# An attention and mixer kernel: pair tiles of the Strassen tail become single PSUM banks, its row additions come in halves, and the order is planned anew

## The chip, the cores and the metric

One core of a Trainium2 chip runs the whole program. The metric is the device time of one execution in microseconds (us). TensorE (PE) multiplies matrices, VectorE (DVE), ScalarE (ACT) and GpSimd (POOL) work element by element, and SyncE (SP) issues all DMA transfers from one queue.

## The reference

Attention with a decay over 64 heads (8 batches of 8 heads, 576 positions, 64 columns), then a mixer over tokens and one over channels:

```python
scores = q @ k.T / sqrt(64) + (cum[i] - cum[j])      # cum: running sum of log(clip(f)); causal
x = softmax(scores) @ v                              # heads side by side: 8 x 576 x 512
u = x + (relu(x.T @ w_tok1) @ w_tok2).T              # 576 -> 256 -> 576
out = u + relu(u @ w_ch1) @ w_ch2                    # 512 -> 1536 -> 512
```

All of it is in 32-bit floats. The kernel splits each operand into a high and a low part of a shorter format (fp32r) and sums three products (high by high, low by high, high by low), so every product of the reference is three matmuls.

## The kernel before, in words

The program has three stages. In **attention** (up to about 560 us) each head's scores are multiplied, reduced, exponentiated, normalised, transposed and multiplied with v, with the token mixer and a first part of the channel mixer woven in. The **conventional part** (to about 693 us) does the channel mixer for 1,024 of the 4,608 tokens. The **tail** does the other 3,584 tokens in four steps of 896 (the function `big`, step s = 0 to 3): each step uses a form of Strassen's scheme in which seven products take the place of eight, once for the way up (512 to 1,536 columns, less the 256 that attention has done) and once for the way down. A product up (the loop over `UP`, L1522 to L1524) has five groups (`pr`) of six matmuls of 448 columns into one PSUM bank each; ACT copies the sum out (L1533), or DVE adds it to a row (L1539). A product down (the function `product`, L1584 to L1586) has five groups of six matmuls: three go to the first half m = 0 of its result and three to the second half m = 1, and the two halves lie in two banks. DVE adds the result to a row of the output in SBUF (L1608, 896 columns; L1604 for the two halves of the very last product). The products of a chain (`CHAIN`) add up in the same banks.

PSUM has eight banks, called b0 to b7 here. b0 and b1 make the tile `pair0`, b2 and b3 `pair1`; attention uses them for scores, results of v and sums. b4 to b7 are the single tiles `bank4` to `bank7` of attention. When attention's single tiles are done, `swapp` lays `pair2` and `pair3` over them. In the tail a sum of the way up is one half of a pair tile (kind `x1`), and a result of the way down is a whole pair tile (kind `x2`). A semaphore wait is placed for a tile, as the framework sees it: a write to a pair tile follows the reads of that pair tile.

The order of the work is not written by hand. A planner (`Plan.run`) simulates the engines with a cost for each operation, and at each moment takes the ready operation of lowest priority number; the numbers stand in the tables `PR`, `OFF`, `STEP` and the like. Its choices fix the order on every engine and which bank each result gets. `dma` gives a transfer a cost on SP's queue (`dur`) and a rate (bytes per ns). Where the plan leaves PE idle, the last loop of the kernel adds small idle matmuls (L783, 16 columns, the operand is the constant `lower`); 120 of them stand at the start:

```python
for _ in range(PRM["FILL"] if at_ == 0 else int((gap - GAP[0]) / GAP[1]) if gap > GAP[2] else 0):
    E["idle"](at_ == 0)
```

At the start SP loads the first heads' q and k (`xt<-in_qk`, L962, for the first four heads, which lie in a tile named xt, and `raw<-in_qk`, L925, for later ones), the decay input (`xt<-in_f`, L751) and the token mixer's weights (`dd<-in_w_tok`, L798). The decay passes DVE and ACT (L752 to L757), and its rows go by DMA beside q and k (`xt<-cc`, L947); the scores (L985) read both.

Of the kernel before, what the change touches and what calls it, by code (L numbers as in the profile page):

```python
# [13 lines left out]
ALU = mybir.AluOpType  # L14
# [9 lines left out]
    k0=(2,),  # L24
    k1=(3,),
# [6 lines left out]
    k8=(1,),  # L32
    k9=(3,),
    k10=(4, 5, 6, 7, 8, 9,),
    k11=(6, 2, 4, 7, 8, 14, 16, 18, 22, 28, 32, 40, 41, 42, 43, 46, 62, 59, 53, 57, 63, 78, 77, 79, 80, 95, 112, 110, 111, 109, 126, 469, 470, 472, 471, 473, 481, 480, 478, 477, 479, 487, 486, 485, 484, 488, 493, 495, 494, 496, 498, 502, 499, 501, 500, 503, 506, 505, 507, 510, 512, 517, 515, 516, 518, 520,),
    k12=(2, 3, 6, 8, 11, 15, 20, 27, 33, 36, 46, 50, 56, 78, 101, 106, 161, 910, 912, 929, 930, 940, 941, 949, 950, 958, 960, 964, 969, 972, 982, 987, 991, 994, 998,),
    k13=(4, 5, 8, 11, 18, 20, 30, 32, 41, 46, 56, 70, 68, 93, 137, 115, 194, 983, 986, 1001, 1003, 1013, 1015, 1024, 1025, 1034, 1038, 1044, 1052, 1055, 1061, 1064, 1069, 1073, 1078,),
    k14=(6, 7, 9, 14, 19, 21, 39, 38, 45, 48, 58, 74, 72, 98, 171, 138, 200, 985, 988, 1004, 1005, 1014, 1017, 1032, 1030, 1036, 1040, 1045, 1054, 1059, 1063, 1065, 1070, 1074, 1079,),
    k16=(4, 5, 9, 13, 18, 19, 35, 34, 39, 40, 53, 66, 65, 98, 156, 906, 905, 915, 918, 935, 936, 947, 946, 959, 956, 961, 963, 967, 977, 984, 988, 989, 992, 996, 1001,),
    k17=(10, 11, 12, 13, 14, 19, 27, 26, 28, 30, 35, 51, 48, 61, 97, 981, 979, 999, 998, 1011, 1012, 1021, 1019, 1035, 1031, 1041, 1046, 1048, 1058, 1062, 1066, 1067, 1071, 1076, 1081,),  # L40
    k18=(12, 19, 48, 61, 72, 74, 89, 106, 120, 136, 154, 169, 181, 192, 206, 222, 240, 249, 266, 283, 295, 309, 315, 336, 347, 362, 384, 388, 399, 420, 433, 444,),
    k19=(10, 11, 20, 15, 21, 23, 34, 36,),
    k20=(0, 5, 27, 33,),
    k21=(0, 2, 1, 5, 4, 3, 11, 13, 9, 22, 18, 23, 30, 29, 25, 38, 36, 35, 49, 50, 53, 59, 60, 57, 75, 80, 77, 89, 93, 90, 103, 104, 106, 114, 116, 115, 135, 137, 134, 144, 151, 146, 170, 168, 167, 184, 181, 187, 198, 200, 201, 217, 214, 216, 227, 229, 228, 240, 242, 241, 260, 264, 262, 277, 276, 275, 293, 295, 292, 305, 315, 312, 324, 330, 327, 342, 343, 345, 359, 362, 361, 371, 380, 373, 389, 392, 394, 406, 408, 403, 421, 420, 425, 437, 440, 438, 453, 454, 456, 469, 466, 470, 487, 489, 485, 498, 500, 499, 522, 517, 519, 538, 533, 537, 553, 555, 551, 565, 569, 568, 579, 585, 600, 605, 607, 606, 618, 623, 621, 632, 644, 637, 653, 668, 658, 675, 673, 670, 700, 697, 702, 705, 709, 704, 723, 720, 722, 739, 742, 735, 760, 763, 762, 766, 764, 772, 799, 797, 800, 807, 813, 805, 817, 820, 831, 833, 837, 828, 847, 861, 860, 863, 862, 875, 880, 892, 889, 901, 896, 902, 915, 918, 922, 929, 925, 931, 949, 948, 951, 961, 964, 952,),
# [413 lines left out]
    ),  # L458
)
F1 = PRM["F1"]  # L460

QUADS = ("11", "12", "21", "22")
HW = 256
GAP = (300, 85, 700)
HT = 448
CONV = 2


def dd_units(a, n):
    return tuple(("dd", i) for i in range(a, a + n))  # L470
# [207 lines left out]
def build(nc, env, dims):  # L678
# [32 lines left out]
    def at(b):  # L711
        return env[b.kind][b.slot]
# [1352 lines left out]
```

## Time and profile before

| what | before |
|---|---|
| median of 3 runs | 1051.08 us (1050.98 to 1052.93) |
| profiled execution, its time | 1053.12 us |
| profiled execution, its span (first to last instruction) | 1050.0 us |
| PE busy in the span | 1030.5 us (98%) |
| DVE, ACT, POOL busy | 77%, 66%, 40% |
| granted TensorE clock, mean | 0.996 |

The span is what the instructions cover; 3.1 us lie around it in the profiled execution. A matmul's record begins when it starts and ends with a modelled end, and neighbours overlap, so the start of the next one tells how fast PE goes. The granted clock is a share of 2.4 GHz: 1.00 is that level, 0.50 is 1.2 GHz.

### The profile page before, as it was taken

To read this page: it belongs to the slowest core of one execution; us is meant where nothing else is said; L and a number is where in the kernel's file an instruction comes from. 1 tells how busy PE (TensorE), PEld (TensorE's weight loads), DVE (VectorE), ACT (ScalarE), POOL (GpSimd) and SP (SyncE) were. 2 spreads that over 40 slices of the span, in tenths; PEclk is the share of its full clock that TensorE was granted. 3 is DMA by queue.
4 is the path that set the end of the run, shared out by engine and by line. 5 is a ranking of instruction groups with operands and counts; after the bars stand their busy time and mean duration, and the time that the engine had idled before them with its cause. 6 is when DMAs were issued, how large, how long until landed. Compare 5 with 4: busy or idle time off the path is not lost.

```text
span 1050.0 us, 19792 instructions
## 1 busy us (share of the span) xinstructions
PE 1030.5 (98%) x6481; PEld 928.9 (88%) x6481; DVE 807.1 (77%) x1943; ACT 689.3 (66%) x1719; POOL 419.2 (40%) x528
## 2 busy tenths in 40 slices
PE   8999999999999999999999999999999999999998
PEld 6678999999999999999999888889898888989897
DVE  5788888888888777888899995456966875786594
ACT  5788888788788878888997542235446544643552
POOL 5478868778788585987942000000000000000000
PEclk9999999999999999999999999999999999999999
DMA  7766657465655545555548845052683284277044
GB/s 216 223 232 212 227 184 235 176 210 187 204 196 196 203 175 173 199 190 200 214 149 274 291 158 184 10 179 82 201 267 114 89 253 150 93 243 226 1 162 158
DMA packets 101605, 192.59 MB, mean 183 GB/s; under 512 B 14032, under 2 KB 45520, under 8 KB 100480
## 3 DMA queue, kind: packets, MB, share of 16 engines
q1 hardware_dynamic: 101504, 191.34, 54.6%
q8 instruction: 51, 0.84, 0.3%
q14 instruction: 50, 0.41, 0.1%
HBM read 100.16 MB, written 37.49 MB: 131 GB/s over the span
## 4 chain that ended last, share of the span: by engine, by line
PE 88%; ACT 4%; DVE 4%; issue 1%; DMA 1%; POOL 1%; SPq 0%; DVEq 0%; ACTq 0%; POOLq 0%
PE bank L1041 10%; PE bank L985 6%; PE pair L1584 5%; PE pair L1585 5%; PE pair L1586 5%; PE pair L1522 5%; PE pair L1524 5%; PE pair L1523 5%; PE pair L985 3%; PE pair L1123 3%; PE pair L1125 3%; PE bank L1256 2%; PE pair L1277 2%; PE bank L1258 2%; PE bank L1257 2%; PE pair L1279 2%
## 5 line engine op out<-in xcount | busy, mean ns | idle before, releaser
L1027 POOL TENSOR_SCALAR pr<-pr,rec 128x448 f32<-128x448 f32 (+4 forms) x320 | 165.2, 532 | 69.8 <-DVE rec L1020 35.4
L719 ACT ACTIVATE p<-bank 128x384 fp32r<-128x384 f32 (+3 forms) x300 | 129.9, 473 | 23.4 <-PE bank L1041 20.8
L1041 PE MATMUL bank<-ident,pr 128*128 128x128 f32 (+1 forms) x960 | 141.4, 276 | 0.8 <-DVE ring L731 0.4
L999 ACT ACTIVATE pr<-bank,nmin 64x64 f32<-64x64 f32 (+3 forms) x256 | 118.3, 468 | 24.7 <-DVE nmin L992 21.7
L1041 PEld LDWEIGHTS bank<-ident,pr 128*128 128x128 f32 (+1 forms) x960 | 107.2, 131 | 21.1 <-issue 3.8
L728 DVE TENSOR_TENSOR p<-bank,p 128x384 fp32r<-128x384 f32 (+1 forms) x180 | 106.0, 591 | 18.1 <-ACT p L719 16.7
L992 DVE CUSTOM_DVE_ANT_0 bank<-bank,mask 64x64 f32<-64x64 f32 (+3 forms) x256 | 107.0, 430 | 12.7 <-PE bank L985 8.5
L1584 PE MATMUL pair<-ring,w2r 128*128 128x448 f32 x230 | 84.6, 368 | 2.3 <-ACT ring L719 0.8
L985 PE MATMUL bank<-k 128*128 128x320 f32 (+1 forms) x480 | 84.8, 304 | 0.8 <-DVE low L728 0.4
L1585 PE MATMUL pair<-ring,w2r 128*128 128x448 f32 x230 | 84.2, 366 | 0.0
L1586 PE MATMUL pair<-ring,w2r 128*128 128x448 f32 x210 | 76.9, 366 | 0.0
L1125 PE MATMUL pair<-p,vv 128*128 128x512 f32 x240 | 76.6, 321 | 0.0
L719 ACT ACTIVATE ring<-xt 128x448 fp32r<-128x448 f32 (+2 forms) x100 | 60.1, 612 | 21.4 <-DVE xt L1734 5.1
L911 POOL TENSOR_TENSOR hl<-raw,hl 128x1152 fp32r<-128x1152 f32 x27 | 72.1, 2669 | 1.6
L1123 PE MATMUL pair<-p,vv 128*64 128x512 f32 x240 | 70.0, 332 | 0.0
L985 PEld LDWEIGHTS bank<-k 128*128 128x128 f32 (+1 forms) x480 | 62.1, 176 | 5.1 <-DVE low L728 0.8
L728 DVE TENSOR_TENSOR low<-bank,p 64x512 fp32r<-64x512 f32 (+1 forms) x120 | 52.4, 443 | 14.1 <-ACT p L719 12.5
L999 ACT ACTIVATE pr<-pair,nmin 128x576 f32<-128x576 f32 x64 | 47.2, 738 | 13.3 <-DVE nmin L992 10.7
L725 POOL TENSOR_TENSOR ring<-xt,ring 128x576 fp32r<-128x576 f32 x32 | 46.3, 1456 | 19.5 <-ACT ring L719 19.3
L722 POOL TENSOR_SCALAR p<-low 64x576 fp32r<-64x576 f32 x60 | 40.1, 668 | 31.6 <-DVE low L728 25.6
L992 DVE CUSTOM_DVE_ANT_0 pair<-pair,mask 128x576 f32<-128x576 f32 x64 | 48.9, 764 | 4.3 <-PE pair L985 4.2
L719 ACT ACTIVATE ring<-bank 128x512 fp32r<-128x512 f32 (+2 forms) x96 | 46.9, 497 | 7.2 <-PE bank L1767 3.7
(202 smaller groups left out, 3156.9 us busy)
## 6 DMA issues: line engine op xcount, KB each, us to landing
k<-hl SPq DMA_DIRECT2D x180, 288.0 KB
w2r<-sd SPq DMA_DIRECT2D x80, 256.0 KB
raw<-in_qk SPq DMA_DIRECT2D x60, 288.0 KB
w2r<-qd SPq DMA_DIRECT2D x60, 256.0 KB
vr<-in_v SPq DMA_DIRECT2D x32, 320.0 KB
ud<-xt SPq DMA_DIRECT2D x8, 1152.0 KB
pd<-part SPq DMA_DIRECT2D x32, 288.0 KB
dd<-in_w_ch SPq DMA_DIRECT2D x12, 512.0 KB
```

The source lines that it names most:

```text
L719: nc.scalar.activation(out, in_, func, scale=scale)
L728: nc.vector.tensor_tensor(out, in_, asf(hi), op=ALU.subtract)
L985: nc.tensor.matmul(ps[:m, of : of + w], k[:, 0, i0 : i0 + m], k[:, 1, j0 : j0 + w], start=(x == 0), stop=(fq or x == 1))
L992: nc.vector.tensor_tensor_reduce(x, x, E["mask"][:m, a : a + w], -1.0 / D**0.5, 3e38, op0=ALU.add, op1=ALU.min, accum_out=E["nmin"][sm][:m ...
L999: nc.scalar.activation(at(pr)[:m, poff[t] : poff[t] + w], at(buf)[:m, of : of + w], AF.Exp, bias=E["nmin"][sm][:m, t : t + 1], scale=-1.0, ...
L1027: nc.gpsimd.tensor_scalar(x, x, r, 0.0, op0=ALU.mult, op1=ALU.add)
L1041: nc.tensor.transpose(out, at(pr)[:, poff[i] + start[j] : poff[i] + end[j]], E["ident"])
L1123: nc.tensor.matmul(x[:D], at(vv)[:, v0 + j, :D], at(pb)[:, 1, c0 : c0 + w], start=False, stop=last)
L1125: nc.tensor.matmul(x, at(vv)[:, v0 + j, :], at(pb)[:, 0, c0 : c0 + w], start=False, stop=last)
L1584: nc.tensor.matmul(o_, wh[:, ms], h_, start=first and pr == 0, stop=False, skip_group_check=not first)
L1585: nc.tensor.matmul(o_, wl[:, ms], h_, start=False, stop=False, skip_group_check=not first)
L1586: nc.tensor.matmul(o_, wh[:, ms], l_, start=False, stop=pr == PH - 1, skip_group_check=not first)
```

## The change

PSUM: b4 to b7 stay single tiles for the whole program, and the pair tiles of b0 to b3 are given up after attention's and the conventional part's last use, for four single tiles (`swapp`). All sums of the tail, up and down, now take single banks: a result of the way down has two of them, any two. The first product up of the first step may take b4 to b7 before that exchange (kind `y1`). The DVE addition of a result is two instructions of 448 columns, one for each bank, in place of one of 896. The store to the output stays one transfer, but for the last product.

Planning: the model's transfers begin no earlier than 2,450 ns; a load of later heads' q and k costs 600 ns of SP's queue (before: 400) and moves at 260 bytes per ns (300), and a gather of a head's operand (`k<-hl`, L958) at 330 (300). Idle matmuls planned before 50,000 ns go by their own thresholds (`EARLY`). The priority tables are replaced as a whole, so the order differs everywhere. Cut to its core:

```diff
-GAP = (300, 85, 700)
+GAP, EARLY = (300, 85, 700), (200, 65, 500)
...
-        tail = dma_at = port_at = 0.0
+        tail = port_at = 0.0
+        dma_at = 2450.0
...
-                    n + o["load"], lambda raw=raw, n=n, x=x: nc.sync.dma_start(at(raw)[x::2], E["qk"][n // 2][x * D : x * D + D]), 294912, dur=400, wr=[(raw, x)], bufs=[raw]
+                    n + o["load"], lambda raw=raw, n=n, x=x: nc.sync.dma_start(at(raw)[x::2], E["qk"][n // 2][x * D : x * D + D]), 294912, dur=600, rate=260, wr=[(raw, x)], bufs=[raw]
...
-            dma(n + o["kh"], lambda k1=k1, f=gather: f(at(k1)[0::2], 0, 2), 294912, dur=660, rd=[(hl, 0)], wr=[(k1, 0)], bufs=[k1, hl])
+            dma(n + o["kh"], lambda k1=k1, f=gather: f(at(k1)[0::2], 0, 2), 294912, dur=660, rate=330, rd=[(hl, 0)], wr=[(k1, 0)], bufs=[k1, hl])
...
-                ps = Buf("x1") if first else held_[ch, pr]
+                ps = Buf("y1" if s == 0 and k == 1 and pr < 4 else "x1") if first else held_[ch, pr]
...
-            ps = Buf("x2") if first else held_[ch]
+            ps = [Buf("x1") for _ in (0, 1)] if first else held_[ch]
...
-                        o_ = res(m)
+                        o_ = at(ps[m])[:, :HT]
...
-                        p.op("PE", [mm_(HT)] * 3, pp if m == 0 else pp + L, lambda f=mm, m=m: f((m,)), rd=b + ([ps] if m else []), wr=[(ps, m)] + ([] if m else [ps]), bufs=[ps, *b])
+                        p.op("PE", [mm_(HT)] * 3, pp if m == 0 else pp + L, lambda f=mm, m=m: f((m,)), rd=b, wr=[ps[m]], bufs=[ps[m], *b])
...
-            p.op("DVE", d_dve(T), tk, lambda: nc.vector.tensor_tensor(Rq(to), res(), Rq(to), op=ALU.add), rd=[ps], wr=[R[to]], bufs=[ps, R[to]])
+            for c in (0, 1):
+                p.op(
+                    "DVE", d_dve(HT), tk, lambda c=c: nc.vector.tensor_tensor(Rq(to)[:, c], at(ps[c])[:, :HT], Rq(to)[:, c], op=ALU.add),
+                    rd=[ps[c], R[to]], wr=[(R[to], "o", c)], bufs=[ps[c], R[to]],
+                )
...
-        if any(z.kind == "one" for z in q.bufs):
+        if any(z.kind in ("sc", "av", "acc") for z in q.bufs):
...
 def swapp():
-        ones.__exit__(None, None, None)
-        pairs.extend(pp.tile([P, 1024], F32, name=f"pair{i}") for i in (2, 3))
+        pairp.__exit__(None, None, None)
+        E["x1"] = {**banks, **{(f"b{i}",): pp.tile([P, 512], F32, name=f"bank{i}") for i in range(4)}}
...
+                g0, g1, g2 = GAP if o.start > 50000 else EARLY
+                for _ in range(PRM["FILL"] if at_ == 0 else int((gap - g0) / g1) if gap > g2 else 0):
```

Three places show what the new plan does. The first is SP's queue at the start of the program, before and then after (`xt_135` holds the decay input f, `xt_136` the first heads' q and k, `raw` later heads' q and k, `dd` weights to be decoded):

```order
L962 DMA xt_136<-in_qk 64x1152
L925 DMA raw_157<-in_qk 64x1152
L798 DMA dd<-in_w_tok 64x512
L751 DMA xt_135<-in_f 64x576
L798 DMA dd<-in_w_tok 128x512
L962 DMA xt_136<-in_qk 64x1152
```

```order
L925 DMA raw_157<-in_qk 64x1152
L751 DMA xt_135<-in_f 64x576
L798 DMA dd<-in_w_tok 64x512
L798 DMA dd<-in_w_tok 128x512
L962 DMA xt_136<-in_qk 64x1152
L798 DMA dd<-in_w_tok 64x512
```

The decay input moves from the fourth place to the second, and the first head's q and k from the first to the fifth.

The second place is PE's start: the idle matmuls (L783), then the scores of the first head (one result in a pair tile, two in bank tiles), idle matmuls, the scores of the second head, before and then after:

```order
L783 MATMUL pair_64<-lower 16x128 x87
L985 MATMUL pair_63<-xt_136 128x288 x2
L985 MATMUL bank_68<-xt_136 128x320
L985 MATMUL bank_68<-xt_136 128x192
L985 MATMUL bank_69<-xt_136 64x64
L985 MATMUL bank_69<-xt_136 128x448
L783 MATMUL pair_64<-lower 16x128 x33
L985 MATMUL bank_68<-xt_136 128x320
L985 MATMUL bank_68<-xt_136 128x192
```

```order
L783 MATMUL pair_71<-lower 16x128 x87
L985 MATMUL pair_70<-xt_136 128x288 x2
L985 MATMUL bank_63<-xt_136 128x320
L985 MATMUL bank_63<-xt_136 128x192
L985 MATMUL bank_64<-xt_136 64x64
L985 MATMUL bank_64<-xt_136 128x448
L783 MATMUL pair_71<-lower 16x128 x18
L985 MATMUL bank_65<-xt_136 128x320
L985 MATMUL bank_65<-xt_136 128x192
```

The second head now gets banks of its own, where before it took the first head's again, and 18 idle matmuls stand ahead of it in place of 33; another 23 follow behind it.

The third place is PE's last product, whose two halves m = 0 and m = 1 are added and stored one by one: before, where the first half ends and the second begins, and after, the last three groups of the program:

```order
L1584 MATMUL pair0_63<-ring8_145,w2r3_7248 128x448
L1585 MATMUL pair0_63<-ring8_145,w2r3_7248 128x448
L1586 MATMUL pair0_63<-w2r5_7252,w2r3_7248 128x448
L1584 MATMUL pair0_63<-ring0_137,w2r4_7250 128x448
L1585 MATMUL pair0_63<-ring0_137,w2r4_7250 128x448
L1586 MATMUL pair0_63<-ring10_147,w2r4_7250 128x448
```

```order
L1584 MATMUL bank5_64<-ring1_138,w2r1_6963 128x448
L1585 MATMUL bank5_64<-ring1_138,w2r1_6963 128x448
L1586 MATMUL bank5_64<-w2r7_7267,w2r1_6963 128x448
L1584 MATMUL bank0_8387<-ring3_140,w2r0_6961 128x448
L1585 MATMUL bank0_8387<-ring3_140,w2r0_6961 128x448
L1586 MATMUL bank0_8387<-ring4_141,w2r0_6961 128x448
L1584 MATMUL bank0_8387<-ring1_138,w2r1_6963 128x448
L1585 MATMUL bank0_8387<-ring1_138,w2r1_6963 128x448
L1586 MATMUL bank0_8387<-w2r7_7267,w2r1_6963 128x448
```

Both halves had the tile `pair0`, in two blocks of 15 matmuls; now each half has its own tile, the halves' groups alternate up to there, and the first half ends six matmuls before the program's last.

## Rows read from the trace of the kernel before

**Rows 1.** The page, part 1: busy time (share) and instructions of each engine.

```profile
PE 1030.5 (98%) x6481; PEld 928.9 (88%) x6481; DVE 807.1 (77%) x1943; ACT 689.3 (66%) x1719; POOL 419.2 (40%) x528
```

**Rows 2.** Stretches: length; PE, PEld, DVE, ACT, POOL busy; granted clock; DMA share, GB/s.

```profile
0.00:12.64 12.64, 11.51 (x126) 9.81 (x126) 4.52 (x17) 4.96 (x8) 8.07 (x18) 1.00 0.73 190
...
21.93:28.76 6.83, 6.83 (x20) 4.75 (x20) 4.22 (x16) 3.60 (x12) 2.79 (x6) 0.50 0.98 277
28.76:62.00 33.24, 33.24 (x170) 19.60 (x168) 25.49 (x84) 27.72 (x82) 19.83 (x34) 1.00 0.68 218
62.00:100.00 38.00, 35.02 (x257) 30.20 (x257) 33.12 (x100) 32.27 (x92) 30.63 (x37) 1.00 0.60 211
100.00:560.00 460.00, 458.85 (x3525) 433.44 (x3524) 383.42 (x1116) 384.23 (x1061) 346.94 (x426) 1.00 0.57 198
...
693.17:1046.40 353.23, 346.30 (x1681) 314.04 (x1679) 250.07 (x394) 174.45 (x332) 0.00 (x0) 1.00 0.51 163
```

**Rows 3.** Timeline of the tail near 813: start, length, what [idle before <-releaser].

```profile
811.91 0.62 DVE L1539 TENSOR_TENSOR dd<-pair,dd 128x448 f32<-128x448 f32 x1 [1.23 <-PE pair L1524]
...
812.52 0.36 PE L1523 MATMUL pair<-ring,held 128*128 128x448 f32 x1
...
812.73 0.36 PE L1524 MATMUL pair<-ring,held 128*128 128x448 f32 x1
...
813.52 0.53 ACT L1533 ACTIVATE dd<-pair 128x448 f32<-128x448 f32 x1
...
814.10 0.47 PE L1522 MATMUL pair<-w2r,held 128*128 128x448 f32 x1 [1.01 <-ACT dd L1533]
```

**Rows 4.** Timeline of the tail near 820.

```profile
819.80 0.62 DVE L1539 TENSOR_TENSOR dd<-pair,dd 128x448 f32<-128x448 f32 x1
...
820.87 0.62 DVE L1539 TENSOR_TENSOR dd<-pair,dd 128x448 f32<-128x448 f32 x1
...
821.54 0.47 PE L1522 MATMUL pair<-w2r,held 128*128 128x448 f32 x1 [0.99 <-DVE dd L1539]
```

**Rows 5.** Timeline of the tail near 891.

```profile
890.74 0.55 ACT L1533 ACTIVATE dd<-pair 128x448 f32<-128x448 f32 x1 [1.45 <-PE pair L1524]
...
892.12 0.53 ACT L1533 ACTIVATE dd<-pair 128x448 f32<-128x448 f32 x1
...
892.70 0.47 PE L1522 MATMUL pair<-ring,held 128*128 128x448 f32 x1 [0.78 <-ACT dd L1533]
```

**Rows 6.** Timeline of the tail near 853.

```profile
852.80 1.08 DVE L1608 TENSOR_TENSOR r<-pair,r 128x896 f32<-128x896 f32 x1
...
853.99 0.44 PE L1584 MATMUL pair<-ring,w2r 128*128 128x448 f32 x1 [0.57 <-DVE r L1608]
```

**Rows 7.** Timeline of the last product.

```profile
1043.03 0.62 DVE L1604 TENSOR_TENSOR r<-pair,r 128x448 f32<-128x448 f32 x1 [1.39 <-PE pair L1586]
...
1043.71 0.47 PE L1584 MATMUL pair<-ring,w2r 128*128 128x448 f32 x1 [0.71 <-DVE r L1604]
```

**Rows 8.** Groups of one line, DVE, tail: count, busy, mean ns, idle before.

```profile
L1608 DVE TENSOR_TENSOR part<-pair,part 128x896 f32<-128x896 f32 x16 | 17.4, 1088 | 5.4 <-PE pair L1586 5.4
```

**Rows 9.** Waits of PE in the tail: us in total, times, longest.

```profile
PE pair L1522 <- ACT mask L1533: 0.6, 1, 0.6
...
PE pair L1584 <- DVE h L1539: 0.2, 1, 0.2
```

**Rows 10.** Timeline of the start: SP's issues (SPq) and PE.

```profile
1.37 0.57 SPq L925 DMA_DIRECT2D raw<-in_qk  x1
...
2.62 0.60 SPq L751 DMA_DIRECT2D xt<-in_f  x1
...
6.97 5.67 PE L783 MATMUL pair<-lower 128*16 128x128 f32 x87
...
13.33 1.21 PE L985 MATMUL pair<-xt 66*128 66x288 f32 x4 [0.69 <-DMA xt<-cc]
...
20.45 3.01 PE L985 MATMUL bank<-xt 66*128 66x320 f32 x8 [1.91 <-ACT held L719]
```

More of the change, by code (lines that the diff above doesn't have):

```diff
@@ L23 @@
 PR = dict(
-    k0=(2,),
-    k1=(3,),
+    k0=(1,),
+    k1=(1,),
     k2=(0,),
@@ L1526, in big @@
                 p.op(
-                    "PE", [mm_(HT)] * 6, pp, mm, rd=[*th, *tl, *toks_of(1, pr, blk)] + ([("turn", s)] if k == 1 else []) + ["gatep"] * (first and s == 0),
+                    "PE", [mm_(HT)] * 6, pp, mm, rd=[*th, *tl, *toks_of(1, pr, blk)] + ([("turn", s)] if k == 1 else []) + ["gatep"] * (first and ps.kind == "x1" and s == 0),
                     wr=[ps], bufs=[ps, *th, *tl],
@@ L1600, in product @@
             tk = t2 + L * (n + 1)
             to = {1: "11", 2: "11", 6: "12", 5: "22", 7: "22", 3: "12", 4: "21"}[k]
-            if ends:
-                for c in (0, 1):
-                    p.op("DVE", d_dve(HT), tk, lambda c=c: nc.vector.tensor_tensor(Rq("21")[:, c], res(c), Rq("21")[:, c], op=ALU.add), rd=[(ps, c), R["21"]], wr=[(R["21"], "o", c)], bufs=[ps, R["21"]])
-                    dst = E["outT"][(2 + c) * P : (3 + c) * P, t0 : t0 + HT]
-                    dma(tk, lambda c=c, dst=dst: nc.sync.dma_start(dst, Rq("21")[:, c]), P * HT * 4, rd=[(R["21"], "o", c)], bufs=[R["21"]])
-                return
@@ L1879, in attn_mixer_kernel @@
     const = ctx.enter_context(tc.tile_pool(name="const", bufs=1))
-    pairs = [psum.tile([P, 1024], F32, name=f"pair{i}") for i in range(2)]
-    ones = tc.tile_pool(name="ones", bufs=1, space=bass.MemoryType.PSUM)
-    op_ = ones.__enter__()
+    banks = {(f"b{i}",): psum.tile([P, 512], F32, name=f"bank{i}") for i in range(4, 8)}
+    E["one"] = E["y1"] = banks
+    pairp = tc.tile_pool(name="pairs", bufs=1, space=bass.MemoryType.PSUM)
+    pp = pairp.__enter__()
+    pairs = [pp.tile([P, 1024], F32, name=f"pair{i}") for i in range(2)]
     E["sc"] = {("b0", "b1"): pairs[0]}
@@ L1886, in attn_mixer_kernel @@
     E["acc"] = {(f"b{i}",): pairs[i // 2][:, (i % 2) * 512 : (i % 2) * 512 + 512] for i in range(4)}
-    E["one"] = {(f"b{i}",): op_.tile([P, 512], F32, name=f"bank{i}") for i in range(4, 8)}
     def swapp():
-        ones.__exit__(None, None, None)
-        pp = ctx.enter_context(tc.tile_pool(name="pairs", bufs=1, space=bass.MemoryType.PSUM, reuse_waits="tile"))
-        pairs.extend(pp.tile([P, 1024], F32, name=f"pair{i}") for i in (2, 3))
-        E["x1"] = {(f"b{i}",): pairs[i // 2][:, (i % 2) * 512 : (i % 2) * 512 + 512] for i in range(8)}
-        E["x2"] = {(f"b{2 * i}", f"b{2 * i + 1}"): x for i, x in enumerate(pairs)}
+        pairp.__exit__(None, None, None)
+        pp = ctx.enter_context(tc.tile_pool(name="lasts", bufs=1, space=bass.MemoryType.PSUM, reuse_waits="tile"))
+        E["x1"] = {**banks, **{(f"b{i}",): pp.tile([P, 512], F32, name=f"bank{i}") for i in range(4)}}
     E["swapp"] = swapp
@@ L2023, in attn_mixer_kernel @@
         for o in order:
-            heads = heads and not any(x.kind in ("acc", "dA", "dB", "x1", "x2") for x in o.bufs)
+            heads = heads and not any(x.kind in ("acc", "x1", "y1") for x in o.bufs)
             if o.eng == "PE":
                 gap = (o.start - at_) * heads
-                for _ in range(PRM["FILL"] if at_ == 0 else int((gap - GAP[0]) / GAP[1]) if gap > GAP[2] else 0):
+                g0, g1, g2 = GAP if o.start > 50000 else EARLY
+                for _ in range(PRM["FILL"] if at_ == 0 else int((gap - g0) / g1) if gap > g2 else 0):
                     E["idle"](at_ == 0)
```

235 lines of the change are left out of this document (118 added, 117 removed).

## The prediction

> **What bounds the kernel now.** I read the page's first part: PE is busy 98% of the span, and no other engine over 77% (PEld is PE's own loading of weights) [rows 1]. So PE sets the time, and the question for each stage is what PE still waits for. The stretches answer it [rows 2]: from 100 to 560 us PE is busy 458.85 of 460.00 us, so attention has almost no idle time to give back. What is left lies at the two ends. In the tail (693.17 to 1046.40 us) PE is busy 346.30 of 353.23 us. Here two matmuls start 0.21 us apart (812.52 and 812.73) while a record lasts 0.36 us [rows 3]; a wait is therefore about 0.15 us longer than the idle time in its row. In the first 100 us PE waits for the first scores and the second head's, runs 6.83 us at a granted clock of 0.50 (21.93 to 28.76 us), and idles 2.98 us between 62 and 100 us [rows 2, 10].
>
> Then I went through PE's long waits of the tail one by one. Three have the same shape. At 812.73 PE starts the last matmul of a group; the next group starts at 814.10, when ACT has read a result at 814.05 [rows 3]. In the plan that group's bank is b3, the second half of `pair1`, whose last reader is the DVE addition that ended at 812.53; the ACT read is of b2, the other half. The profile's rows name only the pair, so which half it is comes from the plan. In the same way the group at 821.54 has b0, free when DVE ended at 820.42, and waits for DVE's reading of b1 until 821.49 [rows 4]; that at 892.70 has b7, free at 891.29, and waits for b6 until 892.65 [rows 5]. The last product shows it without the plan: its second half starts at 1043.71, after DVE has added the first half from 1043.03 to 1043.65, though the two share no bank [rows 7]. The tile is the unit of a wait, and the tile has two banks.
>
> **The tail, part by part.** *Single banks.* The four waits go, since each group's own bank was free in time. From the idle times 1.01 [rows 3], 0.99 [rows 4], 0.78 [rows 5] and 0.71 us [rows 7], with 0.15 us each, less 0.08 us at 820.42 (the bank's true release comes a little after PE could start): 3.49 + 0.60 - 0.08 = 4.0 us. PE is the bound, so what it doesn't wait it gains, unless the operands come next; ACT is busy only 174.45 and DVE 250.07 of 353.23 us there [rows 2], so I count all of it.
>
> *Additions in halves.* At 853.99 PE waits truly: both banks of a result are read by one addition of 1.08 us that starts at 852.80 [rows 6]. One half takes 0.62 us [rows 7]; the first bank is free at 853.42 and its three matmuls cover the reading of the second: 853.99 becomes 853.47, 0.5 us. The price is DVE time: two halves are 1.24 us against 1.09 us [rows 7, 8], 0.15 us for each of 27 additions, 4 us in all. Under it lies DVE's idle time of 103 us in the tail [rows 2], so I cost it at nothing; with that cover gone it would be those 4 us.
>
> A rule speaks against this part. The Trainium skill ("VectorE: DVE Perf Modes", the section on the TRN2 errata) says that an instruction reading SBUF pays a fixed extra latency, and advises tiles of 512 elements or more; 448 is below. By it, with those 4 us on the path, the sum below would be 1 us and not 5. The rows show the fixed cost that the rule speaks of (0.15 us for each cut), but nothing that makes PE pay it.
>
> *The new plan's own waits.* Single banks let the plan take a bank again sooner. I counted in both plans, for each bank that is evicted in the tail and then starts a new sum, how many PE groups stand between its last matmul and the new start: exactly one in 12 cases before and 30 after (two: 46 and 53; beside these, before, the two halves of the last product). One group is six matmuls, 1.24 us. An eviction needs the matmul's end (0.36), about 0.04 to start, 0.62 to read and 0.05 to release, 1.07 us, against 0.21 + 1.24 = 1.45: it fits if the reader comes less than 0.38 us late. Before, two of the 12 show in PE's waits, 0.6 and 0.2 us [rows 9], with the hidden 0.15 each 1.1 us. At that rate 18 more cases cost 1.6 us; with some for second halves, which are read 0.62 us later, I take 2.0. Bounds: nothing, if the plan's timing holds; 18 times the larger wait's half, about 6 us. I take a value near the rate, since ACT and DVE have idle time.
>
> The exchange of tiles needs the last sums of the conventional part to be added first. Before the first group in b0 to b3, five groups in b4 to b7 stand on PE (6 us), more than the additions take; I cost it at nothing. The tail: 4.0 + 0.5 - 2.0 = 2.5 us gained, between 4.5 gained and 1.5 lost.
>
> **The start.** The decay input moves to the place of the second issue: 1.37 in place of 2.62 us [rows 10]. The chain behind it (DVE, ACT, DVE, DMA) ends in the first scores at 13.33 us, after an idle 0.69 us. The 120 idle matmuls end at 6.97 + 5.67 = 12.64 us and stand ahead of the scores in both programs, so of the 1.25 us PE can have 0.69. The first head's q and k, now fifth, have 816 KiB ahead of them and 288 KiB of their own; at the 190 GB/s of this stretch [rows 2] that is 5.9 us behind the first issue, well before 12.64. Nothing is lost there.
>
> PE's second wait ends at 20.45 us after 1.91 us idle [rows 10]. The row names ACT's decoding of a weight, which the scores do not read; they do read rows that SP issues, and the later of these moves from place 21 of its queue to place 20 with one load of v less ahead, on top of the 1.25 us. I take 1.3 us, between nothing and 1.9.
>
> At 0.50 the clock costs half of 6.83 us, 3.4 us [rows 2]. It fell after PE's two idle stretches. Now 18 + 23 idle matmuls stand among the scores in place of 33, and the waits should be shorter; whether the clock then holds no row tells. I take half, 1.7 us. Sum ahead of 29 us: 0.7 + 1.3 + 1.7 = 3.7, between 0 and 6.0. From 28.76 to 62 us PE is busy all 33.24 us, so it passes through; from 62 to 100 us DVE is busy 33.12, ACT 32.27 and POOL 30.63 of 38.00 us [rows 2], and their work has not shrunk. Part comes back as waits there: I keep two thirds, 2.5 us.
>
> **Attention.** Every order there is new, with the same operations. The distances between an eviction and a bank's next use are much the same in both plans (one or two groups in 6.8% of the cases before, 6.0% after, over most of the stage). I take 0, and 3 us either way.
>
> **Sum.** 2.5 (tail) + 2.5 (start) + 0 = 5.0 us. The profiled execution took 1053.12 us with 3.1 us around its span, and is 2.0 us above the median; taken from it the sum gives 1048.1, and from the median 1051.08 gives 1046.1. I say 1046.0 as the median.
>
> **The rivals.** *The start gives nothing back*: DVE, ACT and POOL, at 81 to 87% from 62 to 100 us, take all of it. For it: that stage waits for them now. Against: DVE was busy only 4.52 of the first 12.64 us [rows 2]. Time: 1051.1 - 2.5 = 1048.6.
>
> *All works out*: the clock holds, and the tight reuses do not wait: 4.5 + 6.0 = 10.5, 1040.6.
>
> *The change does not do what it says*: the waits for other halves go, but the 18 tight reuses and second halves take their place at 4 us and more, and the start gives nothing: about 1051. For it: before, the plan too believed that those banks were free.
>
> *Halves on the path*: where DVE is late already, each cut's 0.15 us reaches PE; if all 27 did, 5.0 - 4.0 = 1.0, so 1050.1. Against: DVE's 103 us of idle time. This is how the rule of "VectorE: DVE Perf Modes" in the Trainium skill would bear here.
>
> *Slower: attention waits for its gathers.* The plan now believes that a gather of 294,912 bytes takes 894 ns in place of 983, so it may place scores 89 ns too early. PE has no idle time in that stage to cover it. At 60 heads, 0.15 us each is 9 us: 1055. It decides from 5.0 / 60 = 83 ns a head, about what the plan gained on one gather. Against: attention's DMA engines are busy only 57% [rows 2], and most gathers have time in hand.
>
> **How the numbers follow.** The forecast has 0.47, the start alone lost 0.17, all works out 0.14, no effect 0.07, halves 0.05, slower gathers 0.10. A measurement tells this kernel from no change beyond about 0.2%, 2.1 us. Faster takes the first three, 0.78; same the next two, 0.12; slower 0.10. The range runs from 1040 (all works out) to 1051 (no effect); the slower case is left out. The likeliest case alone spans 1043.5 to 1048.5, by its terms' bounds.
>
> **What would show it.** Right: no wait of PE in the tail ends with a reader of a bank that its group does not write; the last product has no idle time between its halves; first scores at about 12.7 us and the second head's near 19; idle PE in the tail nearer 4 than 7 us. Wrong: PE waits of 0.3 us and more behind halves read second; a clock of 0.50 for as long as before; PE idle in attention on `k<-hl`; PE idle from 62 to 100 us grown by what the start gained.

## The result, and the profile after

The changed kernel takes 1041.67 us (median of 4 runs, 1039.46 to 1045.64) where the kernel before took 1052.01 us beside it (4 runs, 1050.98 to 1057.73). The ratio is 0.9891, with a 95% interval of 0.9859 to 0.9923: 10.3 us less by the medians, 11.5 by the ratio, where the forecast was 5.0 us less. Two later groups of runs give the same kernel 0.9865 [0.9835, 0.9896] and 0.9888 [0.9857, 0.9920]. The direction was right, and the gain is about twice the forecast.

The profiled execution took 1045.64 us (span 1043.5 us) against 1053.12 us before. The first part of its page, which answers to [rows 1]:

```profile
PE 1028.1 (99%) x6489; PEld 930.0 (89%) x6489; DVE 809.2 (78%) x1970; ACT 689.8 (66%) x1719; POOL 420.2 (40%) x528
```

DVE has 27 instructions more, the cut additions, and PE 8 more idle matmuls. The stretches, as in [rows 2]; the last is the tail, from the end of the conventional part's last matmul to the last matmul of all:

```profile
0.00:12.64 12.64, 11.52 (x116) 9.43 (x117) 4.90 (x18) 5.40 (x9) 9.37 (x19) 1.00 0.78 203
21.93:28.76 6.83, 6.83 (x42) 4.51 (x39) 5.17 (x18) 4.82 (x17) 4.70 (x10) 1.00 1.02 307
28.76:62.00 33.24, 32.71 (x174) 19.81 (x172) 24.89 (x83) 29.05 (x86) 19.73 (x30) 1.00 0.60 201
62.00:100.00 38.00, 34.72 (x259) 30.41 (x258) 33.72 (x97) 32.95 (x90) 33.26 (x41) 1.00 0.69 232
100.00:560.00 460.00, 458.99 (x3538) 435.61 (x3537) 387.62 (x1121) 385.87 (x1061) 345.63 (x423) 1.00 0.58 200
690.37:1038.90 348.53, 345.88 (x1680) 315.96 (x1679) 251.57 (x421) 175.39 (x332) 0.00 (x0) 1.00 0.52 164
```

From 21.93 to 28.76 us the granted clock is now 1.00, with 42 matmuls in place of 20. Attention (100 to 560 us) is as full as it was. The tail is 4.6 us shorter, 348.53 in place of 353.1 us. PE's waits in the tail (us in total, times, longest), to be held against [rows 3 to 5] and [rows 9]:

```profile
PE bank L1584 <- DVE h L1539: 2.0, 1, 2.0
PE bank L1522 <- DVE h L1539: 0.6, 1, 0.6
```

By the plan's banks, both waits end with a reader of a bank that the waiting group itself writes; none ends with the reader of a strange bank any more. The last product, as in [rows 7], runs on while DVE adds its first half:

```profile
1037.52 0.36 PE L1584 MATMUL bank<-ring,w2r 128*128 128x448 f32 x1
...
1037.72 0.62 DVE L1599 TENSOR_TENSOR r<-bank,r 128x448 f32<-128x448 f32 x1 [3.10 <-PE bank L1586]
...
1037.72 0.36 PE L1585 MATMUL bank<-ring,w2r 128*128 128x448 f32 x1
```

The start, as in [rows 10] (SP's issue of the first gather, and PE):

```profile
7.42 0.61 SPq L947 DMA_DIRECT2D xt<-cc  x1
...
7.76 5.67 PE L783 MATMUL pair<-lower 128*16 128x128 f32 x87
13.27 1.19 PE L985 MATMUL pair<-xt 66*128 66x288 f32 x4
...
17.68 2.31 PE L985 MATMUL bank<-xt 66*128 66x320 f32 x8
```

The second head's scores stand at 17.68 us in place of 20.45, the first head's at 13.27 in place of 13.33. The one long wait left is new:

```profile
699.74 0.37 PE L1524 MATMUL bank<-ring,w1r 128*128 128x448 f32 x1
...
700.38 1.09 DVE L1477 TENSOR_TENSOR part<-part,xt 128x896 f32<-128x896 f32 x1 [2.18 <-DMA part<-pd]
...
701.39 0.62 DVE L1539 TENSOR_TENSOR h<-bank,h 128x448 f32<-128x448 f32 x1
...
702.11 0.44 PE L1584 MATMUL bank<-ring,w2r 128*128 128x448 f32 x1 [2.01 <-DVE h L1539]
...
703.19 0.57 PE L1585 MATMUL bank<-ring,w2r 128*128 128x448 f32 x1
...
703.56 0.57 PE L1586 MATMUL bank<-ring,w2r 128*128 128x448 f32 x1
```

PE waits for DVE's addition of line 1539. That was free to run, but line 1477 stands ahead of it in DVE's queue and waits 2.18 us for a read-back from memory. Behind the wait the clock is granted at 0.50 for 3.41 us: matmuls start 0.37 us apart in place of 0.20 (the two last rows).

### The profile page after: what moved, and what is told of

It reads as the page before. It is cut to its first block, busy times and chain, and to the rows that moved or that the text cites. A ratio compares the mean times of both kernels' runs of the same rounds, so it can differ in the third digit from the quotient of the medians.

```text
span 1043.5 us, 19849 instructions
## 1 busy us (share of the span) xinstructions
PE 1028.1 (99%) x6489; PEld 930.0 (89%) x6489; DVE 809.2 (78%) x1970; ACT 689.8 (66%) x1719; POOL 420.2 (40%) x528
## 4 chain that ended last, share of the span: by engine, by line
PE 87%; DMA 4%; DVE 4%; ACT 2%; issue 1%; SPq 1%; DVEq 0%; ACTq 0%
PE bank L1041 10%; PE bank L985 6%; PE bank L1584 5%; PE bank L1585 5%; PE bank L1586 5%; PE bank L1522 5%; PE bank L1523 5%; PE bank L1524 5%; PE pair L985 3%; PE pair L1123 3%; PE pair L1125 3%; PE pair L1277 2%; PE pair L1279 2%; PE pair L1113 2%; PE pair L1278 2%; DMA dd<-in_w_ch 2%
## 5 line engine op out<-in xcount | busy, mean ns | idle before, releaser
L1027 POOL TENSOR_SCALAR pr<-pr,rec 64x64 f32<-64x64 f32 (+4 forms) x320 | 164.7, 530 | 65.6 <-DVE rec L1020 32.9
L992 DVE CUSTOM_DVE_ANT_0 bank<-bank,mask 128x320 f32<-128x320 f32 (+3 forms) x256 | 106.8, 433 | 9.3 <-PE bank L985 5.8
L1584 PE MATMUL bank<-ring,w2r 128*128 128x448 f32 x220 | 80.9, 368 | 2.0 <-DVE h L1539 2.0
L1585 PE MATMUL bank<-ring,w2r 128*128 128x448 f32 x220 | 80.8, 367 | 0.0
L1586 PE MATMUL bank<-ring,w2r 128*128 128x448 f32 x210 | 77.2, 367 | 0.0
L728 DVE TENSOR_TENSOR ring<-xt,ring 128x448 fp32r<-128x448 f32 (+1 forms) x62 | 38.3, 629 | 24.6 <-ACT ring L719 22.9
```

What stands on the lines that cost most here:

```text
L728: nc.vector.tensor_tensor(out, in_, asf(hi), op=ALU.subtract)
L992: nc.vector.tensor_tensor_reduce(x, x, E["mask"][:m, a : a + w], -1.0 / D**0.5, 3e38, op0=ALU.add, op1=ALU.min, accum_out=E["nmin"][sm][:m ...
L1027: nc.gpsimd.tensor_scalar(x, x, r, 0.0, op0=ALU.mult, op1=ALU.add)
L1584: nc.tensor.matmul(o_, wh[:, ms], h_, start=first and pr == 0, stop=False, skip_group_check=not first)
L1585: nc.tensor.matmul(o_, wl[:, ms], h_, start=False, stop=False, skip_group_check=not first)
L1586: nc.tensor.matmul(o_, wh[:, ms], l_, start=False, stop=pr == PH - 1, skip_group_check=not first)
```

## The experiments

Theory A: the gain of the tail is that of single banks. (That it is larger than the four waits that I counted, because the pair tile also holds up the readers, I saw only in the first run below.) Theory B: it is the halves of the additions, or the new order. Theory C: the start gains through its first transfers (C1), its order (C2) or the clock (C3). The runs were made in three groups, each beside its own runs of the kernel before, and all ratios are to those; across groups I compare ratios before times.

Profiled executions also differ in something that none of these edits touches: in some stretches matmuls of 448 columns start 206.6 ns apart and not 202.2 (last section). To compare tails I count those matmuls, times 4.4 ns, and take them off. All lengths are from the end of the last matmul of line 1279 to PE's end:

| Kernel | tail, us | matmuls 4.4 ns wider | rest, us |
|---|---|---|---|
| before | 353.08 | 423: 1.9 us | 351.2 |
| changed, three profiles | 348.53, 346.11, 344.66 | 684, 715, 627: 3.0, 3.2, 2.8 us | 345.5, 342.9, 341.9 |
| old order, pairs, halves | 352.26 | 372: 1.6 us | 350.6 |
| old order, single banks | 341.97 | 0 | 342.0 |
| the same, with the new first loads, two kernels below | 347.34, 346.59 | 1352, 1353: 5.9, 6.0 | 341.4, 340.6 |
| new order, pairs for b0 to b3 | 348.34 | 47: 0.2 us | 348.1 |

**Old order, single banks.** The order before, in which at the first use of b0 to b3 in the tail the two pairs give way to single tiles, and each addition of a result is two halves back to back:

```diff
-                r = at(ps).rearrange("p (m x) -> p m x", m=2)[:, :, :HT]
-                return r if c is None else r[:, c, :]
+                return at(ps)[c][:, :HT]
...
-            p.op("DVE", d_dve(T), tk, lambda: nc.vector.tensor_tensor(Rq(to), res(), Rq(to), op=ALU.add), rd=[ps], wr=[R[to]], bufs=[ps, R[to]])
+            p.op("DVE", d_dve(T), tk, lambda: [nc.vector.tensor_tensor(Rq(to)[:, c], res(c), Rq(to)[:, c], op=ALU.add) for c in (0, 1)], rd=[ps], wr=[R[to]], bufs=[ps, R[to]])
...
+        low = {(f"b{i}",): pp.tile([P, 512], F32, name=f"bank{i}") for i in range(4)}
```

> The order of the kernel before on every engine, but in the tail single bank tiles for all sums, and each row addition as two DVE instructions of 448 columns, back to back; start and attention as before. Theory A (waits for the other half of a pair tile): the waits at 812.7, 820.2, 891.6 and 1042.6 us go and that at 853.1 shortens, so PE's idle time from 693 to 1046 us falls from 6.9 to about 3 us and the kernel is 4 to 5 us (0.4%) faster than before. Theory B (the new order makes the tail's gain): the waits only move on to the next operands, and the time is that of before within 1.5 us.

Measured: 1043.95 us, ratio 0.9907 [0.9873, 0.9942], in a group in which the changed kernel took 1039.79 us. Its tail is 11.1 us shorter than before's, with the order unchanged: 1.9 us of that are the wider matmuls of the table, and the other 9.2 us are waits, as the start times of the matmuls show (added up in the section on the prediction). The stretch of its tail:

```profile
697.74:1039.71 341.97, 341.59 (x1681) 314.79 (x1679) 250.62 (x421) 175.79 (x332) 0.00 (x0) 1.00 0.53 168
```

PE idles 0.38 us in it, against 6.9 us in [rows 2]; about 3 us had been expected. Since the four waits of the prediction make only 4.0 us, I looked for the others, from the readers' side. One place in the kernel before, on PE and ACT:

```profile
991.91 0.37 PE L1524 MATMUL pair<-ring,w1r 128*128 128x448 f32 x1
...
993.13 0.36 PE L1524 MATMUL pair<-w2r,held 128*128 128x448 f32 x1
...
993.53 0.54 ACT L1533 ACTIVATE mask<-pair 128x448 f32<-128x448 f32 x1 [1.64 <-PE pair L1524]
...
994.13 0.47 PE L1522 MATMUL pair<-w2r,w1r 128*128 128x448 f32 x1 [0.63 <-ACT mask L1533]
```

The same read with single banks:

```profile
988.68 0.55 ACT L1533 ACTIVATE mask<-bank 128x448 f32<-128x448 f32 x1
...
989.49 0.36 PE L1524 MATMUL bank<-w2r,held 128*128 128x448 f32 x1
...
989.70 0.36 PE L1522 MATMUL bank<-w2r,w1r 128*128 128x448 f32 x1
```

ACT reads b4 (by the plan), which was complete at 992.28 us. It starts at 993.53, 0.04 us after the group that wrote b5, the other half. The next group takes b4 again and waits for ACT. With single banks ACT starts 1.2 us before that same group ends (989.49 + 0.36 us), and PE goes on 0.21 us later, without a wait. By the plan's banks 18 reads of the tail before (beside the last product's) start within 0.08 us of the end of a group in the other half, though their own bank had been complete for some 1.2 us (one for 2.1): 22.8 us of late reading.

**Old order, pairs, halves.** Only the second of the three edits above (the additions as halves), with the pair tiles kept.

> The kernel before, its order and its pair tiles, with each row addition of a full result done as two halves one after the other. Theory A (the waits for the other half of a pair tile, of PE and of the readers alike, are what single banks remove): with the tiles kept, the tail stays at 352 to 355 us and the median within 2 us of before; the 27 cuts of 0.15 us stay under DVE's idle time. Theory B (the halves are what gains, because the first bank is free sooner): 3 us or more faster. Theory B2 (the cut additions reach PE): 2 to 4 us slower.

Measured: 1052.97 us against 1052.62, ratio 1.0008 [0.9988, 1.0029]. Theory B falls for the old order, and theory A stands: the halves alone give nothing that can be measured (0.6 us in the rest of the tail, where two profiles of the changed kernel differ by 1.0). PE's long waits in this tail are those of before:

```profile
PE pair L1522 <- ACT dd L1533: 1.8, 2, 1.0
PE pair L1522 <- DVE dd L1539: 1.0, 1, 1.0
PE pair L1584 <- DVE r L1604: 0.7, 1, 0.7
PE pair L1522 <- ACT mask L1533: 0.6, 1, 0.6
```

The run can't show what halves are worth beside single banks, since with a pair tile PE still waits for both. At the place of [rows 6] the two halves end at 856.41 us, and PE starts at 856.52:

```profile
855.26 1.15 DVE L1608 TENSOR_TENSOR r<-pair,r 128x448 f32<-128x448 f32 x2
...
855.92 0.37 PE L1586 MATMUL pair<-ring,w2r 128*128 128x448 f32 x1
...
856.52 0.44 PE L1584 MATMUL pair<-ring,w2r 128*128 128x448 f32 x1 [0.23 <-issue]
```

PE idles 0.34 us less here than before (0.23 in place of 0.57), because the addition starts sooner, 0.66 us ahead of PE's last matmul and not 0.26 (852.80 and 853.06): DVE was free earlier.

**New order, pairs for b0 to b3.** The changed kernel, its four single tiles replaced by the halves of two pair tiles:

```diff
+        two = [pp.tile([P, 1024], F32, name=f"pair{i}") for i in (2, 3)]
-        E["x1"] = {**banks, **{(f"b{i}",): pp.tile([P, 512], F32, name=f"bank{i}") for i in range(4)}}
+        E["x1"] = {**banks, **{(f"b{i}",): two[i // 2][:, (i % 2) * 512 : (i % 2) * 512 + 512] for i in range(4)}}
```

> The order of the changed kernel, but b0 to b3 of the tail are halves of two pair tiles (b4 to b7 stay single). Theory A: waits for the other half come back for groups in b0 to b3, and the time is 2 to 6 us above the changed kernel's. Theory B: the order carries the gain, and the time is that of the changed kernel within 1 us.

Measured: 1045.84 us, ratio 0.9926 [0.9897, 0.9954], 6.05 us over the changed kernel in the same group, with half of the banks paired again. Both kinds of wait are back, and Theory B falls here too. DVE starts on a half (b0, by the plan, complete at 782.59) when the other half's group ends (784.41), and PE, which takes b0 next, waits for that late reader. At 810.53 PE writes b3, free since 805.94, and waits for DVE's reading of b2.

```profile
784.05 0.36 PE L1524 MATMUL pair<-ring,w1r 128*128 128x448 f32 x1
...
784.45 1.15 DVE L1599 TENSOR_TENSOR r<-pair,r 128x448 f32<-128x448 f32 x2 [2.86 <-PE pair L1524]
...
785.22 0.44 PE L1522 MATMUL pair<-ring,w1r 128*128 128x448 f32 x1 [0.81 <-DVE r L1599]
...
810.53 0.47 PE L1522 MATMUL pair<-w2r,held 128*128 128x448 f32 x1 [0.40 <-DVE dd L1539]
```

**The changed kernel again**, unaltered, in two groups.

> The changed kernel, unaltered, for a second profile beside the runs below. Two theories of the 2.0 us wait of PE at the first product down (702.11 us) and of the clock that falls to 0.50 at 702.77 us: if the order makes the wait, it is there again, within 0.5 us of the same length, in this execution; if it was a matter of one execution, it is gone. In either case the time should lie between 1039 and 1046 us.

> The changed kernel unaltered, on the same chip as the others of this group: 1038 to 1042.

Measured: 1039.79 and 1040.44 us. The 2.0 us wait near 702 us and the fall of the clock behind it are in neither profile (0.26 and 0.27 us there): the order does not make them. In the first profile alone DVE waits there for a read-back.

**Old first loads.** The changed kernel with SP's first ten transfers in the order of before:

```diff
+    head = [("k20", 0), ("k46", 1), ("k11", 1), ("k1", 0), ("k11", 2), ("k20", 1), ("k11", 0), ("k11", 3), ("k11", 4), ("k46", 0)]
+    for i, g in zip(at10, head):
+        order[i] = by[g]
```

> The changed kernel with SP's first ten transfers in the order of before (q and k first, decay input fourth). Theory C (the decay input's place makes the start's gain): the second head's scores start 1.0 to 1.5 us later than 17.68 us, and at 100 us the kernel is 0.5 to 1.3 us behind the changed one. Theory D (the start's gain is from the bank of its own, the filling and the clock): no later than 0.3 us at 100 us, and the time the same within 0.5 us.

Measured: 1041.59 us, ratio 0.9885 [0.9856, 0.9913]; 1.8 us over the changed kernel in the same group, within the intervals. In its profile the second head's scores start at 18.53 us, 0.85 us later than 17.68; a wait of 1.37 us ends at 24.53, and the clock is at 0.50 from 26.19 us for 3.41 us. PE's first product of line 1123 stands at 64.90 us, against 61.27 in the changed kernel's profile of this group, so the delay there is 3.6 us, where theory C had 0.5 to 1.3 at 100 us. Theory D falls by this profile, though the medians alone would not decide it: in the new order these places do count, through the clock too.

**Old order, single banks, new first loads.** The first kernel of this section with the ten transfers in the new order and with the changed kernel's thresholds for idle matmuls in the first 50 us:

```diff
+    head = [("k46", 1), ("k1", 0), ("k11", 1), ("k11", 2), ("k20", 0), ("k11", 0), ("k20", 1), ("k11", 3), ("k11", 4), ("k46", 0)]
-GAP = (300, 85, 700)
+GAP, EARLY = (300, 85, 700), (200, 65, 500)
+                g0, g1, g2 = GAP if o.start > 50000 else EARLY
```

> Before's order with single banks and halves (as in the first such run), and beside it the first ten transfers of SP in the changed kernel's order and the extra idle matmuls of the first 50 us. Theory C1 (the start's gain comes from these ten places and from the clock): 3 to 5 us faster than the old order with single banks alone, first conventional matmul at about 61 us, end near 1038 us in the profile minus the tail's gain: a median of 1036 to 1041. Theory C2 (the whole new order of the first 60 us is needed): less than 1.5 us faster than with single banks alone.

Measured: 1047.73 us, ratio 0.9934 [0.9905, 0.9963], no better than without them (0.9907, in the first group). C1 falls. The profile shows why: a third head's q and k come late, and the clock falls behind that wait. With the old first loads these scores start at 26.75 us, so what was gained ahead of them ends there. PE, and two stretches:

```profile
26.50 2.07 PE L985 MATMUL bank<-xt 66*128 66x320 f32 x4 [2.16 <-DMA xt<-in_qk]
```

```profile
15.00:26.55 11.55, 9.31 (x85) 6.96 (x83) 9.80 (x35) 8.27 (x28) 6.61 (x11) 1.00 0.79 228
26.55:40.20 13.65, 13.65 (x32) 6.85 (x33) 4.98 (x16) 4.69 (x16) 3.03 (x6) 0.50 0.52 152
```

**The same, with that gap filled** by 34 idle matmuls, which shorten no wait for data:

```diff
-                for _ in range(PRM["FILL"] if at_ == 0 else int((gap - g0) / g1) if gap > g2 else 0):
+                for _ in range(PRM["FILL"] if at_ == 0 else 34 if o.grp == ("k21", 8) else int((gap - g0) / g1) if gap > g2 else 0):
```

> Before's order with single banks, the new first ten transfers and the early idle matmuls, and 34 more idle matmuls (some 2.2 us) ahead of the scores that waited 2.16 us for a transfer until 26.50 us. Theory C3 (in the old order the start loses through the clock, which falls after that wait): the granted clock stays at 1.00 from 15 to 60 us, 5 to 7 us come back against the 13.65 us at 0.50 of the run without these 34, and the median is 1037 to 1042, level with the changed kernel within 2 us. Theory C2 (the order itself feeds PE better from 15 to 60 us): the clock holds or not, and the median stays 3 us or more above the changed kernel's.

Measured: 1042.08 us, ratio 0.9896 [0.9867, 0.9925], beside 1040.44 us for the changed kernel. The same stretches as above, now all at 1.00:

```profile
15.00:26.55 11.55, 11.43 (x118) 9.08 (x116) 9.98 (x35) 8.26 (x28) 6.41 (x11) 1.00 0.78 208
26.55:40.20 13.65, 13.39 (x60) 7.63 (x60) 9.00 (x31) 9.50 (x28) 7.30 (x13) 1.00 0.82 246
```

PE's first product of line 1123 stands at 64.22 us in place of 70.39: 6.2 us back, and half of 13.65 us is 6.8. The mean clock of its six executions is 0.997 to 1.000, without the 34 it was 0.993 to 0.995; by the ratios of the two groups the gain is 4.0 us. C3 is shown for the old order: it loses through the clock. Against C2, the old order then stands within 2 us of the new one. Something of C2 is left: the third head's scores start at 26.81 us here and at 22.47 in the changed kernel's profile beside it, and the first product of line 1123 is 2.8 us later (64.22 and 61.38).

**No early idle matmuls.** The changed kernel without its 18 and 23 idle matmuls:

```diff
-                g0, g1, g2 = GAP if o.start > 50000 else EARLY
+                g0, g1, g2 = GAP if o.start > 50000 else (0, 1, 1e9)
```

> The changed kernel without the 18 and 23 idle matmuls among the first heads' scores (the 120 at the start stay). Theory (they keep the clock up): the granted clock falls to 0.50 for 3 us or more between 15 and 45 us, and the median is 1.5 to 5 us above the changed kernel's. Rival (the shorter waits alone keep it): clock 1.00 throughout and the median within 1 us.

Measured: 1043.33 us, ratio 0.9921 [0.9891, 0.9951], 3.5 to 5.9 us over the changed kernel by the ratios (0.9888 and 0.9865 in the other two groups), with intervals that overlap. The mean clock of its six executions is 0.989 to 0.998; that of the changed kernel's twelve in the two groups is 0.998 to 1.000 but for one of 0.993. The clocks go the theory's way more clearly than the times. In the profile the clock falls to 0.50 after PE has been busy 5.97 of 8.52 us:

```profile
15.00:23.52 8.52, 5.97 (x23) 3.44 (x23) 7.02 (x30) 7.38 (x26) 4.36 (x8) 1.00 0.94 291
23.52:26.93 3.41, 3.41 (x14) 2.68 (x13) 2.47 (x7) 1.22 (x5) 2.83 (x7) 0.50 1.04 268
```

**Two small edits to the changed kernel.** The addition of line 1477 that held up DVE near 700 us, moved behind the one that PE waits for; and the same with 90 idle matmuls ahead of the first scores in place of 120:

```diff
+    late = next(o for o in order if o.grp == ("k101", 0))
+    order.remove(late)
+    order.insert(order.index(next(o for o in order if o.grp == ("k106", 1))) + 1, late)
...
-FILL=120
+FILL=90
```

> The changed kernel with the one DVE addition that waits for a read-back moved behind the addition that PE waits for, near 700 us; all 120 idle matmuls kept. Theory: no wait of more than 0.7 us near 700 us and no fall of the clock there; the median is 0.3 to 2 us below the changed kernel's beside it, with no execution above 1042. Rival (that wait came of one late transfer and is mostly absent): no difference beyond 0.3 us.

> The changed kernel with two edits: 90 instead of 120 idle matmuls ahead of the first scores, and the DVE addition that waits for a read-back of two outputs (near 700 us) moved behind the addition that PE waits for. Theory: first scores 1 to 2 us sooner than 13.27 us (they then wait for their gather, not for the idle matmuls), no wait of 2 us near 700 us, in all 0.5 to 3 us faster than the changed kernel. Rival: the clock falls in the longer gap of the start and takes 1.7 us or more back; no gain.

Measured: 1038.87 us, ratio 0.9871 [0.9843, 0.9898], with the first edit; 0.9872 [0.9842, 0.9901] with both. Neither can be told from the changed kernel (0.9888, 0.9865), and one execution with the first edit took 1043.60 us, above the 1042 that was expected as the most. The first scores did not come sooner with 90 idle matmuls. These end at 11.53 us there, and PE waits:

```profile
7.62 3.91 PE L783 MATMUL pair<-lower 128*16 128x128 f32 x57
13.40 1.21 PE L985 MATMUL pair<-xt 66*128 66x288 f32 x4 [1.88 <-DMA xt<-cc]
```

So the gather bounds the first scores there, not the idle matmuls. In two of that kernel's six executions the mean clock was low: 0.993, at 1044.69 us, and 0.980, at 1060.16 us, the second of which the ratio leaves out. That may be the rival's price; the changed kernel has one of 0.993 too (1046.13 us), so it is not shown.

## Why the prediction was right, and where its sizes were off

*What bounds the kernel.* Right: PE, at both ends.

*Single banks, 4.0 us, and additions in halves, 0.5 us: the mis-sized terms.* Together they measured 9.2 us (351.2 before, 342.0 with single banks in the same order), twice the 4.5 forecast. The two runs have the same 1,680 matmuls in the same order, so that their start times can be compared step by step. The four places of the prediction gave 4.6 us, near its 4.0. The step that failed is "Then I went through PE's long waits of the tail one by one". It took only the long ones, and only those that end with a reader. Two short waits have the same cause, 0.48 and 0.25 us late at 969.75 and 990.78 us (own bank free at 968.80 and 990.06); with what follows them they gave 0.9 us. And it took a reader's own time as given, where the reader had itself been held up by the other half: behind such readers stand the waits at 994.13 us, shown above, and at 737.64 us (2.0 us together; four smaller ones, 1.2 us, I did not trace). ACT's and DVE's waits for "PE pair L1524" look natural, since PE does produce what they read; only the group's bank tells that the matmul named is not the producer.

The additions' part of it is 1.7 us, for PE no longer waits at either place where it had waited for a whole addition. One is that of [rows 6]. The other I missed: the row names ACT's decoding, which ends at 940.81, and PE waits in fact for the addition, which ends at 941.12.

```profile
940.04 1.08 DVE L1608 TENSOR_TENSOR r<-pair,r 128x896 f32<-128x896 f32 x1
...
941.23 0.44 PE L1584 MATMUL pair<-ring,w2r 128*128 128x448 f32 x1 [0.84 <-ACT ring L719]
```

How much of the 1.7 us is due to the halves and how much to the tiles stays open, as halves in pair tiles can't show it. Against the sum stand 1.1 us of new waits.

The price of a cut was too high in the prediction: two halves back to back take 1.15 us, as shown above, and not 1.24, against 1.09 us for the whole. DVE's busy time in the tail grows by 1.3 us for 27 cuts (249.91 before, 251.23 with halves in pair tiles), and it stays hidden. So the rule of the Trainium skill ("VectorE: DVE Perf Modes", the section on the TRN2 errata) that speaks for longer tiles did not decide here: with 27 cuts the ratio is 1.0008. The rival of halves on the path, 4 us, falls.

*The new plan's own waits, 2.0 us.* About 0.5 us: the rest of the tail is 342.9 and 341.9 us in the new order, 342.0 in the old one with the same tiles (by its two later profiles about 1.4). So the new order itself gains nothing in the tail. The rate came from two waits [rows 9], and the larger, 0.6 us, was the read of b4 shown above, which the other half held up. In the first profile after, this term was 3.5 us for another reason: a read-back ahead in DVE's queue (2.0 us), and the clock (half of 3.41 us). I had not looked at what stands ahead of an eviction.

*First scores, 0.69 us.* Wrong: 0.06 us in the first profile, and nothing in the other two (13.62 and 13.77 us). The gather is issued 2.4 us sooner (7.42 in place of 9.79 us) and lands no sooner. In one group, the changed kernel and the one with the old first loads issue it at 7.44 and 9.85 us, and PE's wait for it ends at the same time:

```profile
13.62 1.21 PE L985 MATMUL pair<-xt 66*128 66x288 f32 x4 [0.81 <-DMA xt<-cc]
```

```profile
13.61 1.21 PE L985 MATMUL pair<-xt 66*128 66x288 f32 x4 [0.55 <-DMA xt<-cc]
```

I took the time behind the issue as fixed; it grew from some 3.5 to some 6 us, with SP's other transfers underway at the same time. What made it grow was not tried alone.

*The second head's scores, 1.3 us more.* 2.8 us in all at that place, against 2.0 forecast up to there. With the old first loads 0.85 us of them are lost (18.53 us); what makes the rest was not taken apart.

*The clock, 1.7 us (half of 3.4).* Too little: the changed kernel mostly keeps 1.00 (0.998 and more in 11 of 12 executions), so that nearly all of the 3.4 us came back. The profiled execution before was a usual one: over the kernel's 41 executions in the three groups the mean clock was 0.991 to 0.999, with a median of 0.996, which is also the profiled one's. Those at 0.998 and above took 1048.6 to 1052.2 us, those at 0.993 and below 1055.0 to 1058.2 us. Idle matmuls help to keep it (the runs with the gap filled, and without the early ones).

*Two thirds kept, 2.5 us.* Right as a share: ahead of 29 us the terms above give 2.8 + 3.4 = 6.2 us in place of 3.7, and about 4 are kept. The first product of line 1123 comes 4.4 us sooner (61.08 in place of 65.45), the end of the conventional part 3.0 us (690.37, 693.33), or 3.5 and 4.4 us in the other two profiles. PE idles 3.28 us from 62 to 100 us in place of 2.98, so the rival that the start gives all back falls.

*Attention, 0.* Right: from that first product to the end of the conventional part it is 627.9 us before, and 629.3, 628.6 and 627.5 after. PE does not wait for `k<-hl`; the slower rival falls.

*Sum.* Tail: 9.2 - 0.5 = 8.7 us in place of 2.5; start 3 to 4.4 in place of 2.5. That is 12 to 13 us, where the three groups measured 11.5 to 14.2 by their ratios. The direction and the mechanism were right, and the tail's size was not. The rival *All works out* comes nearest with 10.5 us, but by luck: it has 4.5 for the tail and 6.0 for the start.

## What to carry to other kernels

When a tile covers two PSUM banks, look for waits in both directions, the engine that waits for a reader and the reader that waits for a matmul; follow each wait to the bank, not the name, and do it for the short ones too. The Trainium skill ("Perfetto Trace Analysis", the section on matmuls) advises to rotate groups through different banks so that reading one overlaps the next; the trace agrees (PE idles 0.38 us of the tail with single banks and 6.9 with pairs), and adds that where waits are placed by tile the banks must also be tiles of their own. At the start, a gap that can't be closed can still be filled: 2.2 us of idle matmuls were worth 4 us by the ratios and 6 in the profiles.

## What the runs showed of the hardware that was not expected

At a granted clock of 1.00, matmuls of 448 columns start 202.2 ns apart in some stretches of the tail and 206.6 ns in others, 2.2% more. The profile after shows both (start times of consecutive rows):

```profile
860.18 0.36 PE L1585 MATMUL bank<-ring,w2r 128*128 128x448 f32 x1
...
861.40 0.36 PE L1585 MATMUL bank<-w2r,w2r 128*128 128x448 f32 x1
```

```profile
960.06 0.37 PE L1524 MATMUL bank<-w2r,w1r 128*128 128x448 f32 x1
...
961.30 0.37 PE L1586 MATMUL bank<-ring,w2r 128*128 128x448 f32 x1
```

Six steps take 1.22 us at the first place and 1.24 at the second. The wide stretches lie elsewhere in each profile: none with single banks in the old order, from about 765 us to the end with the new first loads (1352 matmuls, 5.9 us). They count as busy, so no view of waits shows them. Their cause stays open, and no run was aimed at it; 0 to 6 us from one profile to the next, they are part of the spread of one kernel's times.

The stretch at 0.50 in the start also varies, with no edit between: 6.83 us in the profiled execution before, and a mean clock of 0.991 to 0.999 over the others. In the old order with the edits above it was 17.07 us (single banks), 13.65 (and new first loads) and 10.24 (pairs, halves).
